# A new program order for the head of an mLSTM with two MoE layers: tables of due times, later gate matmuls, two more table loads

## The chip, the cores and the metric

The kernel runs on one core of one Trainium2 chip. The metric is the device time of one execution in microseconds (us). Five engines work side by side, each through its own list of instructions in order: PE (TensorE, matmuls), DVE (VectorE), ACT (ScalarE), POOL (GpSimd) and SP (SyncE, which here only issues DMAs). An instruction waits on semaphores until the work on other engines that it needs is done, and everything behind it on its engine waits with it.

## The reference

```python
# attention: B=2, H=8, S=768, D=40; state C (D x D) and n (D) for each batch and head
for t in range(S):
    m_new  = maximum(f_gate[t] + m, i_gate[t])
    f_stab = exp(f_gate[t] + m - m_new);  i_stab = exp(i_gate[t] - m_new);  m = m_new
    C = f_stab * C + i_stab * outer(v[t], k[t]);  n = f_stab * n + i_stab * k[t]
    y[t] = sigmoid(o_gate[t]) * (C @ q[t]) / maximum(abs(n . q[t]), 1)
x = y as (1536 tokens, 320)
# first MoE: 320 -> 2048 -> 320;  g(h) = h for h >= 1, 0 for h <= -1, (h + 1)^2 / 4 between
x = g(x @ w_in) @ w_out
# second MoE, the same sizes:  g(h) = max(h, 0) + log1p(exp(-abs(h)))
out = g(x @ w_in) @ w_out
```

## The kernel before

The recurrence is cut into 12 chunks of 64 steps. A chunk n needs a row of decays and gates, four groups of 32 small matmuls on PE, and work on DVE, ACT and POOL between them. In the order of one chunk, with the lines of the kernel before: `bc_n` (L564, PE: the running maxima `m_n`, L556, are spread over partitions by a matmul), the scan that makes the weights `f_n` from it (L590, DVE; L598 for later chunks), `qkp` (L518, PE: q times k), `f_n` times `qkp` (L620, DVE), `pv` (L505, PE: weights times values), the decay on q (L625, DVE: `qx` times `dec`), `inner` (L511, PE: state times q), `stp` (L526, PE: the chunk's part of the state), the denominators (L650, L653), the sigmoid (L645, ACT), sigmoid times denominators and `y_n` (L657, L660, DVE), the state's product with its decay (L669, POOL) and the sum (L678, DVE), and the transposes of `y_n` (L687, PE), which ACT copies out as `xh` (L692, L693) and DVE completes by the low part `xl` (L698, L700). The first matmuls of the MoE read `xh` and `xl`.

The running maxima of all steps come from two scans on DVE (L341: 16x256 for the first four chunks, 16x512 for the rest). The first four chunks (`EARLY = 4`) take their gates from rows on the chip; their decays go to DRAM (L393, `scr_d<-gd`) and come back spread over partitions as `dec` (L581, two tiles `dec0` and `dec1` in turn). The gates of the other eight come from eight matmuls into the PSUM tile D (L422), three subtractions and additions into `late` (L428), two exponentials (L432), a scan (L436), and two writes to DRAM. The exponentials and the sigmoid are in different activation tables, so between L432 and the first sigmoid stands one load of a table (L449).

The weights of the first MoE come in 32 pieces `raw` of 704 KB (ring of two); ACT turns each into `v` (L715, L719), DVE mends it (L726), ACT casts its high part `w` (L738), and DVE or POOL makes the low part (L747). An up-projection of 128 of the 2048 hidden units is eight matmuls (`h`, L767), named here h_0, h_1 and so on; its activation is three instructions (L775, L780, and L784 on DVE, which makes `u`), then the split `gh` (L816) and `gl` (L820), and a down-projection d_0, d_1 and so on of eight matmuls (L836 to L842). The second MoE is built likewise, with a softplus for activation.

The program order on each engine isn't written by hand. Every step is a task (`add`) with an engine, a cost, what it reads and writes, and a due time that is worked back from its successors; a class `Plan` runs a list scheduler over a model of the core (costs, DMA lanes, TensorE's two clock levels), and emits each instruction when the model starts it. 200 matmuls that compute nothing (`fill`, L460, `WARM`) are among the tasks: the scheduler puts them where PE would be idle ahead of the first up-projection. The choice on each engine is

```python
near = [i for i in q if begin[i] <= now]
...
i = min(near, key=lambda i: (due[i], i))
```

so a change of a due time, of a cost or of the time from which a task is `ready` can move everything behind it.

Of the kernel before, what the change touches and what calls it, by code (L numbers as in the profile page):

```python
# [20 lines left out]
C = 64  # L21
NC = S // C
# [13 lines left out]
class Plan:  # L36
# [44 lines left out]
    def run(self, start):  # L81
# [45 lines left out]
        for i in reversed(order):  # L127
            c = ts[i]["cost"] + ts[i]["after"] + self.LATENCY
            low = min((due[k] for k in succ[i]), default=clock) - c
            due[i] = low if due[i] is None else min(due[i], low)  # L130
        left = [len(d) for d in deps]
        ready = [t["hold"] for t in ts]
        queue, free = {}, {e: 0.55 for e in ("pe", "dve", "act", "pool", "sp")}
# [76 lines left out]
def mlstm_moe_moe(ctx: ExitStack, tc: tile.TileContext, gates, late, qk, tok, ident, w1, w2, out):  # L210
# [126 lines left out]
    for s, (c0, c1) in enumerate(SEG):  # L337
        a, b = c0 * C, c1 * C

        def t(a=a, b=b):  # L340
            nc.vector.tensor_tensor_scan(  # L341
                out=tiles["gm",][:, a + 1:b + 1], data0=gate("gf", a, b), data1=gate("gi", a, b),
                initial=tiles["gm",][:, a:a + 1], op0=ALU.add, op1=ALU.max)
        add("dve", scan(b - a), t, reads=[(gf, s), (gi, s), (gm, "z"), (gm, 0)], writes=[(gm, s)])

# [69 lines left out]

    def t():
        nc.vector.memset(col(4), 0.0)
    add("dve", 0.1, t, reads=[(LT, 0)], writes=[(LT, 4)])

    def t():  # L420
        for c in range(NC - EARLY):
            nc.tensor.matmul(  # L422
                banks[1][:, 2, 0:C + 1], tiles["gi",][0:16, S + 112 - 16 * c:S + 240 - 16 * c],
                tiles["gm",][:, n0 + C * c:n0 + C * c + C + 1], start=(c == 0), stop=(c == NC - EARLY - 1))
    add("pe", 0.9, t, duty=0.75, reads=[(gm, 1), (gm, 0), (gi, 1), (("bc", 1),)], writes=[(("D",), "s")], at=-50.5)
    for k, m, op in ((0, 0, ALU.add), (0, 1, ALU.subtract), (1, 1, ALU.subtract)):
        def t(k=k, m=m, op=op):
            nc.vector.tensor_tensor(out=col(k), in0=col(k), in1=banks[1][:, 2, m:m + C], op=op)  # L428
        add("dve", vec(C), t, reads=[(("D",), "s")], writes=[(LT, k)])
    for k in range(2):  # L430
        def t(k=k):
            nc.scalar.activation(out=col(k), in_=col(k), func=ACTF.Exp)  # L432
        add("act", act(C), t, reads=TAB, writes=[(LT, k)])

    def t():
        nc.vector.tensor_tensor_scan(  # L436
            out=col(5), data0=col(0), data1=col(4), initial=1.0, op0=ALU.mult, op1=ALU.add)
    add("dve", scan(C), t, reads=[(LT, 0), (LT, 4)], writes=[(LT, 5)])

    def t():  # L440
        nc.vector.memset(tiles[LT][:, 0:1], 0.0)
    add("dve", 0.07, t, reads=[(LT, 5)], writes=[(LT, 0)])
    for k, x, key in ((5, scr_d[1], (("scd",), 1)), (0, scr_f, (("scf",),))):
        def t(k=k, x=x):
            nc.sync.dma_start(out=x.rearrange("c r l -> (c r) l"), in_=col(k))
        add("sp", emit=t, reads=[(LT, k)], writes=[key], **dma(32))

    def t():
        nc.scalar.preload_act_table_set("sigmoid_and_others")  # L449
    add("act", 1.3, t, writes=TAB, due=20.0)  # L450


    def t():
# [88 lines left out]
    def attention(c, at):  # L542
# [79 lines left out]
        if c > 0:  # L622
            def t():
                q = tiles[QD][:, 1:3].rearrange("p b i l -> p (b i) l")
                nc.vector.tensor_tensor(out=q, in0=q, in1=tiles[DK], op=ALU.mult)  # L625
            add("dve", vec(512), t, port=True, reads=[*ATT, (DK,)], writes=[(QD,)])

# [28 lines left out]
        def t():  # L656
            nc.vector.scalar_tensor_tensor(  # L657
                out=hd(tiles[SG]), in0=tiles[DN].to_broadcast([128, H, D]), scalar=1.0, in1=hd(tiles[SG]),
                op0=ALU.min, op1=ALU.mult)
            nc.vector.tensor_tensor(  # L660
                out=new("y", Y, [128, DM]).rearrange("p (c i d) -> p c i d", c=2, d=D), in0=pv_view(n)[:, :, :, 0:D],
                in1=tiles[SG].rearrange("p (c i d) -> p c i d", c=2, d=D), op=ALU.mult)
        add("dve", 2 * vec(DM) + 0.1, t, port=True, reads=[*ATT, (P, "p"), (DN,)], writes=[(SG,), (Y, 0)],
            new=[("y", Y)])

# [38 lines left out]
    def weights(l, f):  # L704
# [17 lines left out]
        add("act", act(WC), t, reads=TAB, writes=[(V,)])  # L722

# [32 lines left out]
    def up(l, j, f, at):  # L756
# [3 lines left out]
        def t():  # L760
# [50 lines left out]
    def split_g(l, j, f, G):  # L811
# [6 lines left out]

        def t():
            nc.vector.tensor_tensor(  # L820
                out=new("gl", GL, [128, n], F32R), in0=tiles[G], in1=tiles[GH].bitcast(F32), op=ALU.subtract)
        add("dve", vec(n), t, port=True, reads=[(G,), (GH,)], writes=[(GL,)], new=[("gl", GL)])

    ACC, MIX = ("D",), ("A",)

    def down1(j, f, at):
# [5 lines left out]
        def t():  # L832
# [5 lines left out]
            for i in range(2):  # L838
# [41 lines left out]
    def down2(j, f, at):  # L880
# [181 lines left out]
```

## Time and profile before

| | us |
|---|---|
| time, median of 3 runs (lowest to highest) | 431.64 (430.56 to 433.64) |
| time of the profiled execution | 431.35 |
| its span in the profile | 429.5 |
| mean granted clock of TensorE over the span | 0.991 of full |

The span is the stretch from the first to the last instruction in the profile; the time of the same execution is 1.85 us longer. "Busy" is the time in which an engine worked on data; a matmul in the timeline has its start and its length, and in square brackets the time in which the engine stood idle before it and what ended that. The granted clock is a share of full speed; one half of it is TensorE's lower level.

### The profile page before, as it was taken

To read this page: it belongs to the slowest core of one execution; us is meant where nothing else is said; L and a number is where in the kernel's file an instruction comes from. 1 tells how busy PE (TensorE), PEld (TensorE's weight loads), DVE (VectorE), ACT (ScalarE), POOL (GpSimd) and SP (SyncE) were. 2 spreads that over 40 slices of the span, in tenths; PEclk is the share of its full clock that TensorE was granted. 3 is DMA by queue.
4 is the path that set the end of the run, shared out by engine and by line. 5 is a ranking of instruction groups with operands and counts; after the bars stand their busy time and mean duration, and the time that the engine had idled before them with its cause. 6 is when DMAs were issued, how large, how long until landed. Compare 5 with 4: busy or idle time off the path is not lost.

```text
span 429.5 us, 8096 instructions
## 1 busy us (share of the span) xinstructions
PE 409.7 (95%) x3299; PEld 340.3 (79%) x3299; DVE 295.2 (69%) x479; ACT 260.1 (61%) x447; POOL 37.2 (9%) x46
## 2 busy tenths in 40 slices
PE   7988779999899999999999999999999999999994
PEld 5555558877788888887888888999989999899994
DVE  4687998999868556556878787655565555655552
ACT  3255867768666446889889755555555555555551
POOL 3333122213101000000000000000000000000001
PEclk9999969999999999999999999999999999999999
DMA  8979595797912001644344000000020000110002
GB/s 289 343 260 318 156 295 177 213 321 221 304 66 74 2 2 51 193 162 136 134 134 137 0 2 0 1 2 0 2 61 2 0 2 0 36 27 2 0 2 61
DMA packets 13685, 44.93 MB, mean 105 GB/s; under 512 B 2320, under 2 KB 3984, under 8 KB 13648
## 3 DMA queue, kind: packets, MB, share of 16 engines
q1 hardware_dynamic: 12832, 43.22, 31.2%
q10 hardware_dynamic: 752, 1.03, 0.9%
q8 instruction: 26, 0.43, 0.4%
q0 software_dynamic: 64, 0.16, 0.2%
q14 instruction: 11, 0.09, 0.1%
HBM read 42.36 MB, written 2.05 MB: 103 GB/s over the span
## 4 chain that ended last, share of the span: by engine, by line
PE 77%; DMA 8%; DVE 6%; ACT 4%; issue 1%; SPq 1%; POOL 0%; DVEq 0%; POOLq 0%
PE h L767 36%; DMA raw<-in_w_dram 5%; PE D L841 4%; PE D L840 4%; PE D L842 4%; PE D L897 3%; PE D L899 3%; PE D L898 3%; PE A L898 3%; PE A L899 3%; PE A L897 3%; PE D L836 2%; PE D L837 2%; DMA f<-scr_f 2%; ACT v L715 1%
## 5 line engine op out<-in xcount | busy, mean ns | idle before, releaser
L767 PE MATMUL h<-xh,w 128*128 128x512 f32 x576 | 182.6, 400 | 1.5 <-DVE w L747 1.1
L767 PEld LDWEIGHTS h<-xh,w 128*128 128x128 f32 x576 | 108.7, 189 | 26.8 <-DVE w L747 3.0
L820 DVE TENSOR_TENSOR gl<-u,gh 128x512 fp32r<-128x512 f32 x96 | 67.5, 704 | 39.6 <-ACT gh L816 38.4
L816 ACT CAST gh<-u 128x512 fp32r<-128x512 f32 x96 | 59.4, 619 | 46.7 <-DVE u L807 34.0
L767 PE MATMUL h<-xl,w 128*128 128x512 f32 x192 | 76.3, 397 | 1.4 <-DVE xl L698 1.4
L807 DVE TENSOR_TENSOR u<-u,e 128x512 f32<-128x512 f32 x48 | 33.3, 693 | 29.2 <-ACT e L803 29.2
L803 ACT ACTIVATE e<-e 128x512 f32<-128x512 f32 x48 | 30.3, 632 | 37.6 <-DVE e L798 37.6
L775 ACT ACTIVATE u<-h 128x512 f32<-128x512 f32 x48 | 28.5, 595 | 25.9 <-PE h L767 25.6
L767 PEld LDWEIGHTS h<-xl,w 128*128 128x128 f32 x192 | 36.4, 190 | 8.0 <-DVE xl L698 1.8
L784 DVE SCALAR_TENSOR_TENSOR u<-u,h 128x512 f32<-128x512 f32 x48 | 32.7, 682 | 13.9 <-ACT u L780 13.7
L841 PE MATMUL D<-gh,w 128*128 128x512 f32 x96 | 37.9, 395 | 0.0
L840 PE MATMUL D<-gh,w 128*128 128x512 f32 x96 | 37.8, 394 | 0.0
L842 PE MATMUL D<-gl,w 128*128 128x512 f32 x96 | 37.5, 391 | 0.0
L798 DVE SCALAR_TENSOR_TENSOR e<-u,h 128x512 f32<-128x512 f32 x48 | 33.0, 687 | 6.0 <-ACT u L794 1.0
L726 DVE SCALAR_TENSOR_TENSOR v<-raw,v 128x704 int32<-128x704 int32 x32 | 28.6, 895 | 9.8 <-ACT v L719 8.8
L794 ACT ACTIVATE u<-h 128x512 f32<-128x512 f32 x48 | 28.7, 598 | 10.6 <-PE h L767 10.3
L747 DVE TENSOR_TENSOR w<-v,w 128x64 fp32r<-128x64 f32 (+2 forms) x45 | 30.2, 701 | 2.4 <-ACT w L738 2.4
L715 ACT ACTIVATE v<-raw 128x704 f32<-128x704 int8 x32 | 27.1, 849 | 7.3 <-DMA raw<-in_w_dram 5.4
L780 ACT ACTIVATE u<-u 128x512 f32<-128x512 f32 x48 | 30.2, 630 | 0.4
L897 PE MATMUL D<-w,gh 128*128 128x320 f32 x96 | 29.6, 309 | 0.1
L899 PE MATMUL D<-w,gl 128*128 128x320 f32 x96 | 29.7, 309 | 0.0
L898 PE MATMUL A<-w,gh 128*128 128x320 f32 x96 | 29.7, 309 | 0.0
(120 smaller groups left out, 611.5 us busy)
## 6 DMA issues: line engine op xcount, KB each, us to landing
raw<-in_w_dram SPq DMA_DIRECT2D x32, 704.0 KB, 4.8
qx<-in_qk_dram SPq DMA_DIRECT2D x12, 640.0 KB, 7.2
tok<-in_tok_dram SPq DMA_DIRECT2D x12, 496.0 KB, 6.0
dec<-scr_d SPq DMA_DIRECT2D x16, 128.0 KB, 6.7
f<-scr_f SPq DMA_DIRECT2D x16, 128.0 KB, 6.7
out_dram<-o SPq DMA_DIRECT2D x20, 80.0 KB, 2.1
dec<-scr_d ACTq DMA_DIRECT2D x6, 128.0 KB, 7.0
consts<-in_ident_dram SPq DMA_DIRECT2D x1, 164.0 KB, 4.0
```

Of the source, the lines that this page charges most:

```text
L767: nc.tensor.matmul(hp, a, x, start=(i == 0), stop=(i == len(ops) - 1))
L784: nc.vector.scalar_tensor_tensor(out=tiles[U], in0=tiles[U], scalar=1.0, in1=tiles[HP], op0=ALU.min, op1=ALU.max)
L798: nc.vector.scalar_tensor_tensor(out=new("e", E, [128, n]), in0=tiles[M], scalar=-2.0, in1=tiles[HP], op0=ALU.mult, op1=ALU.add)
L807: nc.vector.tensor_tensor(out=tiles[M], in0=tiles[M], in1=tiles[E], op=ALU.add)
L816: nc.scalar.copy(new("gh", GH, [128, n], F32R), tiles[G])
L820: nc.vector.tensor_tensor(out=new("gl", GL, [128, n], F32R), in0=tiles[G], in1=tiles[GH].bitcast(F32), op=ALU.subtract)
L840: nc.tensor.matmul(d[i], hi[:, k], gh, start=s, stop=False)
L841: nc.tensor.matmul(d[i], lo[:, k], gh, start=False, stop=False)
L842: nc.tensor.matmul(d[i], hi[:, k], gl, start=False, stop=e)
L897: nc.tensor.matmul(d, gh[:, k], hi, start=s, stop=False)
L898: nc.tensor.matmul(d, gh[:, k], lo, start=False, stop=False)
L899: nc.tensor.matmul(d, gl[:, k], hi, start=False, stop=e)
```

## The change

Two tables are added to the planner: `RANK` moves the due times of 41 tasks by up to 7.9 us either way, and `HOLD` the earliest starts of eight. Some costs of the model change (a fill, up- and down-projections, transposes, the late gate matmuls). The second scan of the maxima is held back to 7.6 us of the model's time. The block of the late gates becomes a function that is called ahead of chunk 3 and brings its own table load, so that ACT loads three tables where it loaded one after the first: sigmoid, exponentials, sigmoid. `warm`, which the fills read, is set on DVE and not on POOL. The weights of the first MoE no longer depend on the loaded table. The decay on q (L625) and `gl` (L820) may run on POOL, and sigmoid times denominators and `y` become two tasks.

```diff
+    RANK = {
+        10: 4.3, 19: -7.7, 230: -3.2, 245: 4.3, 248: -7.4, 249: -4.6, 268: 4.6, 280: 1.4, 287: -6.6, 291: 4.4,
...
+    HOLD = {
+        238: 6.2, 258: -4.8, 282: -5.2, 317: 5.5, 318: 7.3, 331: -4.9, 437: 5.0, 438: -2.9,
...
+        for i, d in self.RANK.items():
+            due[i] += d
...
-        ready = [t["hold"] for t in ts]
+        ready = [t["hold"] + self.HOLD.get(t["i"], 0.0) for t in ts]
...
-        add("dve", scan(b - a), t, reads=[(gf, s), (gi, s), (gm, "z"), (gm, 0)], writes=[(gm, s)])
+        add("dve", scan(b - a), t, reads=[(gf, s), (gi, s), (gm, "z"), (gm, 0)], writes=[(gm, s)], hold=7.6 * s)
...
-    add("pe", 0.9, t, duty=0.75, reads=[(gm, 1), (gm, 0), (gi, 1), (("bc", 1),)], writes=[(("D",), "s")], at=-50.5)
...
-    def t():
-        nc.scalar.preload_act_table_set("sigmoid_and_others")
-    add("act", 1.3, t, writes=TAB, due=20.0)
-
-
-    def t():
-        nc.gpsimd.memset(warm, 1.0)
-    add("pool", 0.46, t, writes=[(("warm",),)])
+    def table(name, hold=0.0):
+        def t():
+            nc.scalar.preload_act_table_set(name)
+        add("act", 1.3, t, writes=TAB, hold=hold)
+
+    table("sigmoid_and_others", 7.5)
+
+    def late_gates():
+        table("exp_and_others")
...
+        add("pe", 1.8, t, duty=0.75, reads=[(gm, 1), (gm, 0), (gi, 1)], writes=[(("D",), "s")], at=-30.5, hold=15.0)
...
+        table("sigmoid_and_others")
+
+
+    def t():
+        nc.vector.memset(warm, 1.0)
+    add("dve", 0.1, t, writes=[(("warm",),)])
...
-        add("pe", 0.25, t, fill=True, reads=[(("warm",),)], writes=[(("fill",),)], new=[("hb", ("fill",))] if i == 0 else [])
+        add("pe", 0.215, t, fill=True, reads=[(("warm",),)], writes=[(("fill",),)], new=[("hb", ("fill",))] if i == 0 else [])
...
-            add("dve", vec(512), t, port=True, reads=[*ATT, (DK,)], writes=[(QD,)])
+            add("dve|pool", vec(512), t, port=True, reads=[*ATT, (DK,)], writes=[(QD,)])
...
-        add("pe", 0.34, t, reads=[(Y, 0)], writes=[(TR,), (P, "s")], at=at[3])
+        add("pe", 0.45, t, reads=[(Y, 0)], writes=[(TR,), (P, "s")], at=at[3])
...
-        add("act", act(WC), t, reads=[(R,), *TAB] + ([*ATT] if l else []), writes=[(V,)], new=[(tag, V)])
+        add("act", act(WC), t, reads=[(R,)] + ([*ATT, *TAB] if l else []), writes=[(V,)], new=[(tag, V)])
...
-        add("pe", 8 * (n / 2400 + 0.013), t, reads=[(W, 0), (W, 1)] + xkeys(j), writes=[(HP,)], new=[(tag, HP)], at=at)
+        add("pe", 8 * (n / 2400 + 0.0185), t, reads=[(W, 0), (W, 1)] + xkeys(j), writes=[(HP,)], new=[(tag, HP)], at=at)
...
-        add("dve", vec(n), t, port=True, reads=[(G,), (GH,)], writes=[(GL,)], new=[("gl", GL)])
+        add("dve|pool", vec(n), t, port=True, reads=[(G,), (GH,)], writes=[(GL,)], new=[("gl", GL)])
...
     for n in range(NC):
+        if n == EARLY - 1:
+            late_gates()
         if n == EARLY:
             late_is()
         attention(n, where[n])
```

The lines of the changed kernel have other numbers: by 13 to 21 higher than before.

On ACT, from the cast of `gr` to the first sigmoids (`is_col` holds the gates as columns, `state` the first copy of the state), the kernel before has

```order
L378 CAST gr_128<-gf_142 16x256
L405 COPY is_col_129<-isp_0_200 64x2x8 x4
L393 DMA scr_d0_137<-gd_197 16x4x64
L581 DMA dec0_120<-scr_d0_137 64x512 x2
L581 DMA dec1_121<-scr_d0_137 64x512 x2
L432 ACTIVATE late_164<-late_164 128x64
L676 COPY state_130<-A_122 128x328
L432 ACTIVATE late_164<-late_164 128x64
L449 ACT_TABLE_LOAD
L645 ACTIVATE sig_0_339<-tok_0_155 128x320
```

and the changed kernel

```order
L391 CAST gr_128<-gf_142 16x256
L325 CAST sel_126<-consts_124 128x128
L418 COPY is_col_129<-isp_0_203 64x2x8 x4
L338 COPY id_h_125<-consts_124 128x512
L431 ACT_TABLE_LOAD
L664 ACTIVATE sig_0_240<-tok_0_160 128x320
L406 DMA scr_d0_137<-gd_201 16x4x64
L600 DMA dec0_120<-scr_d0_137 64x512 x2
L697 COPY state_130<-A_122 128x328
L664 ACTIVATE sig_1_322<-tok_1_208 128x320
L600 DMA dec1_121<-scr_d0_137 64x512 x2
```

The table load, a copy (`id_h`) and the first sigmoid now stand ahead of the decays' way to DRAM; the copy of the state and a sigmoid stand between the two pairs of `dec`; the exponentials of `late` have gone to a later place, behind `v` of the second weight.

On PE the eight gate matmuls (L422) stood before `bc_0`:

```order
L518 MATMUL A_122<-qx_0_151 64x64 x16
L399 MATMUL isp_0_200<-consts_124,gi_143 128x16 x2
L422 MATMUL D_123<-gm_148,gi_143 128x65 x8
L460 LDWEIGHTS warm_127
L460 MATMUL fill_162<-warm_127 128x512
L564 MATMUL bc_0_224<-m_0_216,sel_126 128x512
```

and are now in chunk 3 (there L444, between `inner` of chunk 2 and `pv` of chunk 3):

```order
L708 MATMUL D_123<-consts_124,y_1_481 64x128
L537 MATMUL D_123<-qx_3_310 64x64 x16
L530 MATMUL A_122<-state_130,qx_2_170 64x41 x16
L479 LDWEIGHTS warm_127
L479 MATMUL fill_151<-warm_127 128x512
L479 LDWEIGHTS warm_127
L479 MATMUL fill_151<-warm_127 128x512
L444 MATMUL D_123<-gm_148,gi_143 128x65 x8
L524 MATMUL D_123<-vi_3_454,f_3_381 64x41 x16
```

They moved behind the `xl` reads of tile D by chunk 1's transposes, and `pv` of chunk 3 follows them at once.

On PE, ahead of the transposes of chunk 4 (tr_4: L687, in the changed kernel L708), the kernel before has one up-projection, h_3, behind chunk 4's four groups, which stand behind h_0, h_1, h_2 and d_0:

```order
L505 MATMUL A_122<-vi_4_687,f_4_668 64x41 x16
L511 MATMUL A_122<-state_130,qx_4_446 64x41 x16
L518 MATMUL A_122<-qx_5_586 64x64 x16
L526 MATMUL A_122<-ve_4_758,tok_4_482 40x41 x16
L767 MATMUL h_0_0_3_852<-xh0_131,w_0_3_761 128x512
L767 MATMUL h_0_0_3_852<-xl0_134,w_0_3_761 128x512
L767 MATMUL h_0_0_3_852<-xh0_131,w_0_3_761 128x512 x2
L767 MATMUL h_0_0_3_852<-xl0_134,w_0_3_761 128x512
L767 MATMUL h_0_0_3_852<-xh0_131,w_0_3_761 128x512 x3
L687 MATMUL A_122<-consts_124,y_4_874 128x128 x2
```

In the changed kernel chunk 4's groups stand behind h_0 to h_3, d_0 and d_1, and d_2, h_5 and h_4 follow them before tr_4; its end is

```order
L863 MATMUL D_123<-gl_0_0_2_886,w_0_2_688 128x512
L788 MATMUL h_0_0_5_921<-xh0_131,w_0_5_892 128x512
L788 MATMUL h_0_0_5_921<-xl0_134,w_0_5_892 128x512
L788 MATMUL h_0_0_5_921<-xh0_131,w_0_5_892 128x512 x2
L788 MATMUL h_0_0_5_921<-xl0_134,w_0_5_892 128x512
L788 MATMUL h_0_0_5_921<-xh0_131,w_0_5_892 128x512 x3
L788 MATMUL h_0_0_4_935<-xh0_131,w_0_4_811 128x512
L788 MATMUL h_0_0_4_935<-xl0_134,w_0_4_811 128x512
L788 MATMUL h_0_0_4_935<-xh0_131,w_0_4_811 128x512 x2
L788 MATMUL h_0_0_4_935<-xl0_134,w_0_4_811 128x512
L788 MATMUL h_0_0_4_935<-xh0_131,w_0_4_811 128x512 x3
L708 MATMUL A_122<-consts_124,y_4_947 128x128 x2
```

So one up-projection and one down-projection more than before stand between `stp` of chunk 4 and tr_4, and one of each more ahead of chunk 4. Further on in the first MoE the same blocks are in other places too; later the order on PE is the same in both kernels.

## Rows read from the trace of the kernel before

**Rows 1.** The page, parts 1 and 2: engines' totals; granted clock in 40 slices.

```profile
PE 409.7 (95%) x3299; PEld 340.3 (79%) x3299; DVE 295.2 (69%) x479; ACT 260.1 (61%) x447; POOL 37.2 (9%) x46
...
PEclk9999969999999999999999999999999999999999
```

**Rows 2.** Three stretches: busy us of PE, PEld, DVE, ACT, POOL, then granted clock.

```profile
55.00:60.00 5.00, 2.81 (x8) 2.33 (x9) 4.85 (x9) 3.25 (x7) 1.59 (x3) 0.63 0.97 343
60.00:65.00 5.00, 5.00 (x17) 3.96 (x16) 4.96 (x10) 3.06 (x6) 0.00 (x0) 0.69 0.99 263
40.00:115.00 75.00, 67.59 (x868) 53.12 (x867) 66.16 (x115) 55.34 (x95) 14.95 (x15) 0.95 0.76 239
```

**Rows 3.** The waits of PE: us in total, times, the longest.

```profile
PE A L687 <- DVE state L678: 3.8, 2, 2.8
PE A L505 <- DVE f L620: 2.2, 2, 2.0
PE h L767 <- DVE xl L698: 1.4, 1, 1.4
PE h L767 <- DVE w L747: 1.1, 1, 1.1
```

**Rows 4.** PE's timeline up to 60 us: start, length, instruction.

```profile
1.92 2.32 PE L460 MATMUL fill<-warm 128*128 128x512 bf16 x5 [1.92 <-POOL warm L454]
...
6.57 3.65 PE L422 MATMUL D<-gm,gi 16*128 16x65 f32 x16
...
15.33 1.15 PE L526 MATMUL A<-ve,tok 64*64 64x41 f32 x32
...
24.51 0.68 PE L505 MATMUL A<-vi,f 64*64 64x41 f32 x32 [0.21 <-DVE f L620]
...
39.35 0.50 PE L767 MATMUL h<-xl,w 128*128 128x512 f32 x1 [1.36 <-DVE xl L698]
...
50.01 0.68 PE L505 MATMUL A<-vi,f 64*64 64x41 f32 x32 [1.96 <-DVE f L620]
...
57.19 0.90 PE L687 MATMUL A<-consts,y 128*128 128x128 f32 x3 [2.85 <-DVE state L678]
```

**Rows 5.** ACT's timeline up to 20 us.

```profile
7.41 0.34 ACTq L393 DMA_DIRECT2D scr_d<-gd  x1
...
12.66 2.51 ACTq L581 DMA_DIRECT2D dec<-scr_d  x4
...
16.52 0.43 ACT L676 COPY state<-A 128x328 f32<-128x328 f32 x1 [0.29 <-PE A L526]
...
17.12 1.28 ACT L449 ACT_TABLE_LOAD   x1
18.41 0.83 ACT L645 ACTIVATE sig<-tok 128x320 f32<-128x320 f32 x2
```

**Rows 6.** DVE's timeline up to 50 us.

```profile
15.78 0.54 DVE L428 TENSOR_TENSOR late<-late,D 128x64 f32<-128x64 f32 x3
...
21.77 1.21 DVE L590 TENSOR_TENSOR_SCAN f<-bc,id_h 128x512 f32<-128x512 f32 x1
22.90 0.67 DVE L625 TENSOR_TENSOR qx<-qx,dec 128x512 f32<-128x512 f32 x1
...
35.99 2.21 DVE L747 TENSOR_TENSOR w<-v,w 128x64 fp32r<-128x64 f32 x2
...
49.87 0.95 DVE L747 TENSOR_TENSOR w<-v,w 128x64 fp32r<-128x64 f32 x2
```

**Rows 7.** DMAs of `dec`: us from issue to landing.

```profile
DMA to landing us min/median/max: 4.4/6.6/9.3
```

**Rows 8.** DMA issues: queue, count, KB each, median us to landing.

```profile
scr_d<-gd ACTq DMA_DIRECT2D x1, 16.0 KB, 5.2
```

**Rows 9.** POOL's timeline, 30 to 50 us.

```profile
34.97 1.86 POOL L747 TENSOR_TENSOR w<-v,w 128x64 fp32r<-128x64 f32 x2 [0.17 <-ACT w L738]
```

**Rows 10.** The chain that ended last, 125 to 135 us.

```profile
129.88 1.87 PE h L767 x8
```

More of the change, by code (lines that the diff above doesn't have):

```diff
@@ L52 @@
     KEEP, IDLE = 0.8, 0.1
+    RANK = {
[5 rows of a table added]
+    }
+    HOLD = {
+        238: 6.2, 258: -4.8, 282: -5.2, 317: 5.5, 318: 7.3, 331: -4.9, 437: 5.0, 438: -2.9,
+    }
     def __init__(self, bufs):
@@ L414, in mlstm_moe_moe @@
     add("sp", emit=t, writes=[(LT, 0), (LT, 1)], new=[("w", LT)], **dma(64, "late"))
-    def t():
-        nc.vector.memset(col(4), 0.0)
-    add("dve", 0.1, t, reads=[(LT, 0)], writes=[(LT, 4)])
-    def t():
[L421 to L424, printed above, removed]
-    add("pe", 0.9, t, duty=0.75, reads=[(gm, 1), (gm, 0), (gi, 1), (("bc", 1),)], writes=[(("D",), "s")], at=-50.5)
@@ L426, in mlstm_moe_moe @@
[L426 to L433, printed above, removed]
-    def t():
-        nc.vector.tensor_tensor_scan(
-            out=col(5), data0=col(0), data1=col(4), initial=1.0, op0=ALU.mult, op1=ALU.add)
@@ L438, in mlstm_moe_moe @@
[L438 to L448, printed above, removed]
-        nc.scalar.preload_act_table_set("sigmoid_and_others")
@@ L450, in mlstm_moe_moe, with t @@
-    add("act", 1.3, t, writes=TAB, due=20.0)
-    def t():
-        nc.gpsimd.memset(warm, 1.0)
-    add("pool", 0.46, t, writes=[(("warm",),)])
+    def table(name, hold=0.0):
[6 more added lines that the diff above has]
+        def t():
+            nc.vector.memset(col(4), 0.0)
+        add("dve", 0.1, t, reads=[(LT, 0)], writes=[(LT, 4)])
+        def t():
+            for c in range(NC - EARLY):
+                nc.tensor.matmul(
+                    banks[1][:, 2, 0:C + 1], tiles["gi",][0:16, S + 112 - 16 * c:S + 240 - 16 * c],
+                    tiles["gm",][:, n0 + C * c:n0 + C * c + C + 1], start=(c == 0), stop=(c == NC - EARLY - 1))
+        add("pe", 1.8, t, duty=0.75, reads=[(gm, 1), (gm, 0), (gi, 1)], writes=[(("D",), "s")], at=-30.5, hold=15.0)
+        for k, m, op in ((0, 0, ALU.add), (0, 1, ALU.subtract), (1, 1, ALU.subtract)):
+            def t(k=k, m=m, op=op):
+                nc.vector.tensor_tensor(out=col(k), in0=col(k), in1=banks[1][:, 2, m:m + C], op=op)
+            add("dve", vec(C), t, reads=[(("D",), "s")], writes=[(LT, k)])
+        for k in range(2):
+            def t(k=k):
+                nc.scalar.activation(out=col(k), in_=col(k), func=ACTF.Exp)
+            add("act", act(C), t, reads=TAB, writes=[(LT, k)])
+        def t():
+            nc.vector.tensor_tensor_scan(
+                out=col(5), data0=col(0), data1=col(4), initial=1.0, op0=ALU.mult, op1=ALU.add)
+        add("dve", scan(C), t, reads=[(LT, 0), (LT, 4)], writes=[(LT, 5)])
+        def t():
+            nc.vector.memset(tiles[LT][:, 0:1], 0.0)
+        add("dve", 0.07, t, reads=[(LT, 5)], writes=[(LT, 0)])
+        for k, x, key in ((5, scr_d[1], (("scd",), 1)), (0, scr_f, (("scf",),))):
+            def t(k=k, x=x):
+                nc.sync.dma_start(out=x.rearrange("c r l -> (c r) l"), in_=col(k))
+            add("sp", emit=t, reads=[(LT, k)], writes=[key], **dma(32))
+        table("sigmoid_and_others")
@@ L622, in attention, with t @@
         if c > 0:
-            def t():
+            def t(e):
                 q = tiles[QD][:, 1:3].rearrange("p b i l -> p (b i) l")
-                nc.vector.tensor_tensor(out=q, in0=q, in1=tiles[DK], op=ALU.mult)
-            add("dve", vec(512), t, port=True, reads=[*ATT, (DK,)], writes=[(QD,)])
+                (nc.gpsimd if e == "pool" else nc.vector).tensor_tensor(out=q, in0=q, in1=tiles[DK], op=ALU.mult)
+            add("dve|pool", vec(512), t, port=True, reads=[*ATT, (DK,)], writes=[(QD,)])
         if not last:
@@ L659, in t @@
                 op0=ALU.min, op1=ALU.mult)
+        add("dve", vec(DM), t, port=True, reads=[*ATT, (DN,)], writes=[(SG,)])
+        def t():
             nc.vector.tensor_tensor(
@@ L662, in t @@
                 in1=tiles[SG].rearrange("p (c i d) -> p c i d", c=2, d=D), op=ALU.mult)
-        add("dve", 2 * vec(DM) + 0.1, t, port=True, reads=[*ATT, (P, "p"), (DN,)], writes=[(SG,), (Y, 0)],
-            new=[("y", Y)])
+        add("dve", vec(DM) + 0.03, t, reads=[*ATT, (P, "p"), (SG,)], writes=[(Y, 0)], new=[("y", Y)])
         if not last:
@@ L721, in t @@
                 alpha=2.0 ** 40)
-        add("act", act(WC), t, reads=TAB, writes=[(V,)])
+        add("act", act(WC), t, reads=TAB if l else (), writes=[(V,)])
         def t():
@@ L817, in split_g, with t @@
         add("act", act(n), t, reads=[(G,)], writes=[(GH,)], new=[("gh", GH)])
-        def t():
-            nc.vector.tensor_tensor(
+        def t(e):
+            (nc.gpsimd if e == "pool" else nc.vector).tensor_tensor(
                 out=new("gl", GL, [128, n], F32R), in0=tiles[G], in1=tiles[GH].bitcast(F32), op=ALU.subtract)
-        add("dve", vec(n), t, port=True, reads=[(G,), (GH,)], writes=[(GL,)], new=[("gl", GL)])
+        add("dve|pool", vec(n), t, port=True, reads=[(G,), (GH,)], writes=[(GL,)], new=[("gl", GL)])
     ACC, MIX = ("D",), ("A",)
@@ L842, in t @@
                 nc.tensor.matmul(d[i], hi[:, k], gl, start=False, stop=e)
-        add("pe", 8 * (n / 2400 + 0.013), t, reads=[(W, 0), (W, 1), (GH,), (GL,)], writes=[(ACC, i) for i in [0, 1, 2, *("qps" if first else "")]], at=at)
+        add("pe", 8 * (n / 2400 + 0.0185), t, reads=[(W, 0), (W, 1), (GH,), (GL,)], writes=[(ACC, i) for i in [0, 1, 2, *("qps" if first else "")]], at=at)
     def to_x(j):
@@ L899, in t @@
                 nc.tensor.matmul(d, gl[:, k], hi, start=False, stop=e)
-        add("pe", m * 3 * (DM / 2400 + 0.013), t, reads=[(W, 0), (W, 1), (GH,), (GL,)], writes=dk, at=at)
+        add("pe", m * 3 * (DM / 2400 + 0.0167), t, reads=[(W, 0), (W, 1), (GH,), (GL,)], writes=dk, at=at)
         if e:
```

4 rows, old and new, of the table RANK are left out of this document.

## The prediction

> **What bounds the kernel now.** I read the page first: PE is busy for 409.7 us of 429.5, and the granted clock is at its full level in 39 of 40 slices; the one that stands apart is the sixth, 54 to 64 us [rows 1]. So time can come only from PE's idle stretches and from that slice. The stretches say where: from 40 to 115 us PE is busy 67.59 of 75 us and VectorE 66.16 [rows 2], while behind that PE has almost no gaps (the whole list of PE's waits, of which [rows 3] are the largest, is short). So the change, which moves the first 60 us and a little of what follows, can win in two places: before the first up-projection gets going, at 39.35, where its wait for `xl` ends [rows 4], and between there and 115.
>
> What may be won after 39.35: PE waited 1.96 us for f_4's product at 50.01 and 2.85 us for state_4 at 57.19 [rows 4]; the group of L687 has one more wait, 3.8 less 2.8 = 1.0, and L767 waited 1.1 for a weight [rows 3]. That is 6.9 us. Then the clock: at 57.19 PE went back to work after 2.85 idle, and the granted clock of 55 to 60 is 0.63 and of 60 to 65 0.69 [rows 2]. At its lower level (one half) a share of 0.31 lost in the second stretch is 5 x 0.31 / 0.5 = 3.1 us, so the low clock ends near 63.1; from 57.19 that is 5.9 us in which 2.95 us of full-speed work were done. So 2.95 are lost. Together 9.85 us is the most that this stretch can give by its waits.
>
> What may be won before 39.35: the way to it goes over the decays. scr_d is issued at 7.41, its data lands 5.2 us later, at 12.6, and dec is issued at 12.66 (four in 2.51 us) [rows 5, 8]; dec takes 4.4 to 9.3 us to land [rows 7]; qx times dec of chunk 1 starts at 22.90 [rows 6]. Behind it on VectorE stand the products of chunks 1 to 3, whose y, transposes, xh and xl release the first up-projection.
>
> **The change part by part: the head.** On ACT the table load (1.28 [rows 5]) and sigma_0 now stand ahead of scr_d. The queue that issues DMAs is held up by the wait of sigma_0 for tok_0; I put the issue at 8.0 instead of 7.41 (an estimate: the load begins where is_col ended, near 7.8, and the DMA needs no result of it). Landing 5.2 later is 13.2, dec0 is issued at 13.3 and 13.9. The next copy (state, 0.43 [rows 5]) stands behind that pair and before the pair dec1, so dec1 no longer shares the lanes with dec0, and raw1 now waits for dec0 on SP. Landing by the middle value, 6.6, less a little for the emptier queues: 19.9; by the ends, 18.3 and 23.2 [rows 7]. The state's copy was at 16.52 because two `late` exponentials stood around it, whose input needed L422; these have gone. den_0, f_2's scan and y_0 then end by 17.5, and qx of chunk 1 starts at 19.9, 3.0 us before its old start.
>
> From there to the first xl, VectorE has other work than before. Ahead of qx stood f_3's scan (1.21) and the three `late` steps (0.54) [rows 6]; now they stand behind it, and so does the product of f_1 (at the length of the qx row, 0.67): +2.4. Against it, w_0's low part leaves VectorE for POOL: -0.95 by its ordinary row, -2.21 by the row at 35.99 [rows 6]; I take -1.3. The eight gate matmuls, 3.65 us at the lower clock [rows 4], now stand in chunk 3 with the product of f_3 waiting for them on VectorE, and v's mend, den_3, y_3 and all of xl behind that product. At full clock they cost half, 1.8, and fills stand ahead of them, so I take 1.4 exposed; the bounds are 0 (xh and the transposes of chunk 1 fill it) and 3.65. Two more table loads of 1.28 on ACT stand before v_0's second step and before sigma_3; in the order they lie between steps that wait for the first weights and for y, so I count them as hidden by those waits; if sigma_3 comes last behind them, they cost up to one load, 1.28. Sum of the head: -3.0 + 2.4 - 1.3 + 1.4 = -0.5. With the ends: the dec row moves it by -1.6 or +3.3, the gates by -1.4 or +2.2, so about -2.3 to +2.9 where not all fall on one side. More fills from the first microsecond (11 ahead of qk0 instead of 5, first start 1.92 [rows 4]) cost nothing where PE waits anyway for qx; the cover is that wait. If it is gone, six fills at 0.46 each (2.32 / 5) are 2.8.
>
> **After the first up-projection.** Before, chunk 4's four groups stood behind h_0 to h_2 and d_0, and only h_3 between its last group and its transposes. An up- or down-projection is 1.87 us [rows 10], a chunk's group 0.68 [rows 4]. So PE had 5 x 1.87 + 4 x 0.68 = 12.1 us of work where it took 57.19 - 39.35 = 17.8. Now it has h_0 to h_5 and d_0 to d_2 ahead of the transposes: 9 x 1.87 + 2.7 = 19.5 us. VectorE's work in 40 to 57 was 13.7 us, and one more hinge and one more split at 0.69 each make 15.1. So PE's work is longer than VectorE's here, and the 2.85 us wait with its 2.95 us of low clock has nothing to stand on: -5.8. The 1.96 us wait for f_4: chunk 4 is two blocks later, 3.7 us; the wait goes unless f_4's scan comes later too, which waits for dec, scr_f and two DMAs behind it that the later gates push back. I leave as much here: what PE gains in one place it waits in another, w_3, gl_0 or f_4, since VectorE now has 0.9 of its time full. So 2.0 stay here, and the two late waits (1.0 and 1.1) stay as well: 9.85 - 4.1 = 5.75 won, with bounds 0 (VectorE is the bound, below) and 9.85.
>
> POOL takes over qx of five chunks and gl of three blocks, at 0.68 each of VectorE's time, 5.4 us, about three of them in its fullest stretch. But the row says what a move may cost: while POOL worked on w_1 for 1.86 us from 34.97 [rows 9], VectorE's own w took 2.21 instead of 0.95 [rows 6]. That is 1.26 us for one neighbour. The Trainium skill, "SBUF — State Buffer", section on the two separate sides, says that VectorE and GpSimd share one port pair under an exclusive lock, so that an instruction with two SBUF inputs on VectorE stands still while GpSimd has it; the row agrees, and by that rule alone the eight moves, at 1.86 x 512 / 704 = 1.35 us each on POOL by the row, would cost up to 10.8 us of VectorE's time to free 5.4, which is rival C. Between that and a gain of 5.4 I take the moves at zero, since POOL is busy for 15 of the 75 us [rows 2] and many of VectorE's neighbours read PSUM.
>
> **The sum.** 431.35 (the profiled execution) - 0.5 - 5.75 = 425.1. The run is 0.3 below the median of three, and I don't correct for that.
>
> **The rivals.** (A) As above, 425.1: 0.45. (B) As above, but the gate matmuls and groups of chunk 3 come at the lower clock or dec lands late: +2.9 + 0.5 in place of -0.5 for the head, 428 to 429: 0.17. (C) VectorE is the bound: it is busy 66.16 of 75 us [rows 2], what PE does earlier it then waits for, and POOL's work holds it up as in [rows 6, 9]; then most of the 5.75 comes back as waits for u and gl, 429 to 431.6: 0.16. This is also the case in which the new order doesn't do what it is made for. (D) Slower: dec0 lands after 9.3 us, at 23.2, and PE, idle meanwhile, falls to the lower clock in the head: seven groups cost 1.15 instead of 0.68 (3.3), the gates 3.65 instead of 1.8, and qx starts 0.3 later than before instead of 3.0 earlier. 3.3 + 1.8 + 3.3 - 0.5 = +7.9 for the head, with half of what follows won (-3): 436; it decides from a landing of dec0 after 23 us. 432.5 to 438: 0.12. (E) Better: the late waits vanish as well (-2.1), and the head wins 2.3: 421.2: 0.10.
>
> A table load may cost ACT more than its 1.28: the sigmoid follows it at 18.41, where 17.12 + 1.28 ends [rows 5], so the row shows none. The Trainium skill, "ScalarE: Activation LUTs", section on what ACT_TABLE_LOAD costs, gives 2.66 us with a drain; by that, the two added loads would stand 2.7 us longer on ACT, of which I would expect half before xh, so some 426.5; the row speaks against the drain, and that this holds has a chance of 0.05, which lies inside A and B.
>
> **How the numbers follow.** The forecast is A, 425.1. The range leaves out about 1 in 10 on each side: below, E's outer half, so 420.5; above, D, so 432.5. A measurement of this kernel tells 1% (4.3 us) from no change. Faster than 427.3: A but a little of its upper edge (0.43), E (0.10) and the edge of B (0.03): 0.56. Within 1%, 427.3 to 436: the rest of B, C and a part of D: 0.34. Slower than 436: 0.10.
>
> **What would show it.** In the profile after: qx of chunk 1 on VectorE near 19.9; the gate matmuls near 30 us at 1.8 us, not 3.65; the first `xl` matmul of the MoE near 38.9; no wait of PE above 1 us before chunk 4's transposes and full clock in 55 to 65; one wait near 50 us of about 2 us. It is wrong if dec0 lands after 23, if the clock falls before 40 us, or if PE's waits for VectorE from 40 to 115 us sum up to more than 6.

## The result, and the profile after

The changed kernel is slower: 434.31 us in the median of 19 runs (431.67 to 436.85) against 430.99 of the kernel before (19 runs, 428.98 to 437.39), a ratio of 1.0073 with an interval of 1.0049 to 1.0097. That is less than the 1% that I took as a bound, but clear of noise. The forecast was 425.1, with a range of 420.5 to 432.5. Medians here and below are over all runs; ratios and their intervals leave out runs more than 1.5% above the fastest of the same kernel. The profiled execution took 435.12, its span is 433.3.

The page, parts 1 and 2 [rows 1]:

```profile
PE 413.9 (96%) x3313; PEld 341.8 (79%) x3313; DVE 292.8 (68%) x473; ACT 263.9 (61%) x449; POOL 47.4 (11%) x52
...
PEclk9956899999999999999999999999999999999999
```

The slice at 54 to 64 us that stood apart before is full now, as forecast; but the third to fifth, 22 to 54 us, are low. In all 19 runs the mean granted clock is 0.965 to 0.981. Stretches of 2 and 5 us say when (columns as in [rows 2]):

```profile
20.00:22.00 2.00, 0.08 (x4) 0.00 (x0) 0.29 (x1) 1.97 (x3) 0.00 (x0) 0.95 0.08 25
22.00:24.00 2.00, 0.94 (x36) 0.95 (x40) 2.00 (x3) 0.29 (x1) 0.00 (x0) 0.50 0.83 290
...
32.00:34.00 2.00, 1.55 (x52) 1.00 (x48) 0.95 (x4) 1.59 (x4) 1.59 (x2) 0.99 1.02 399
...
36.00:38.00 2.00, 1.09 (x32) 0.94 (x32) 1.19 (x3) 0.00 (x0) 0.15 (x1) 0.50 0.01 4
...
55.00:60.00 5.00, 4.46 (x18) 3.40 (x19) 4.44 (x7) 4.94 (x10) 0.91 (x1) 1.00 0.91 234
```

PE was idle from 20 to 23; from 22 the clock is at its lower level, comes back at 32, falls again at 35.5, during the gate matmuls (33.75 to 35.88), and is back at 45.7. One thing these rows don't show: the low clock of the first microseconds. In the kernel before the five fills at 1.92 take 2.32 us [rows 4], 0.46 each, and six fills at 34.74 take 1.46, 0.24 each, though its row for 5 to 10 us shows full clock. So a mean granted clock says nothing about the very start. PE's timeline shows what it waited for, and the new times of the places in [rows 4]:

```profile
19.39 0.68 PE L537 MATMUL A<-qx 40*64 40x64 f32 x30
23.05 1.10 PE L524 MATMUL D<-vi,f 64*64 64x41 f32 x32 [2.98 <-DVE f L639]
...
33.75 2.13 PE L444 MATMUL D<-gm,gi 16*128 16x65 f32 x16 [0.45 <-DVE xh L721]
36.73 1.09 PE L524 MATMUL D<-vi,f 64*64 64x41 f32 x32 [0.85 <-DVE f L639]
...
47.54 0.40 PE L788 MATMUL h<-xl,w 128*128 128x512 f32 x1
```

The wait of 2.98 us belongs to pv of chunk 1, for f_1's product. On VectorE that product stands behind the decay on q, which waits for dec0 [rows 6]:

```profile
21.71 0.69 DVE L644 TENSOR_TENSOR qx<-qx,dec 128x512 f32<-128x512 f32 x1 [3.86 <-DMA dec<-scr_d]
22.32 0.68 DVE L639 TENSOR_TENSOR f<-D,f 128x512 f32<-128x512 f32 x1
```

The two parts of the time come apart at the first `xl` matmul: 47.54 instead of 39.35, so the head is 8.2 us longer; from there to the end of the span it is 385.8 us instead of 390.15, 4.4 shorter. Between 47 and 120 us the largest waits, in the place of [rows 3], are now these (behind 120 one more of 1.0 for `w`):

```profile
PE A L708 <- DVE f L639: 1.9, 1, 1.9
PE h L788 <- DVE u L805: 0.8, 1, 0.8
...
PE h L788 <- DVE w L768: 0.3, 1, 0.3
```

### The profile page after: what moved, and what is told of

It reads as the page before. It is cut to its first block, busy times and chain, and to the rows that moved or that the text cites. A ratio compares the mean times of both kernels' runs of the same rounds, so it can differ in the third digit from the quotient of the medians.

```text
span 433.3 us, 8123 instructions
## 1 busy us (share of the span) xinstructions
PE 413.9 (96%) x3313; PEld 341.8 (79%) x3313; DVE 292.8 (68%) x473; ACT 263.9 (61%) x449; POOL 47.4 (11%) x52
## 4 chain that ended last, share of the span: by engine, by line
PE 76%; DMA 9%; DVE 8%; ACT 4%; issue 1%; SPq 1%; POOL 0%; ACTq 0%; DVEq 0%; POOLq 0%
PE h L788 35%; DMA raw<-in_w_dram 4%; PE D L862 4%; PE D L861 4%; PE D L863 4%; DMA dec<-scr_d 3%; PE A L919 3%; PE D L919 3%; PE D L920 3%; PE A L920 3%; PE D L918 3%; PE A L918 3%; PE D L857 2%; DVE w L768 2%; PE D L858 2%; PE fill L479 2%
## 5 line engine op out<-in xcount | busy, mean ns | idle before, releaser
L841 DVE TENSOR_TENSOR gl<-u,gh 128x512 fp32r<-128x512 f32 x93 | 64.8, 697 | 37.4 <-ACT gh L837 37.0
L828 DVE TENSOR_TENSOR u<-u,e 128x512 f32<-128x512 f32 x48 | 33.2, 693 | 29.2 <-ACT e L824 29.2
L796 ACT ACTIVATE u<-h 128x512 f32<-128x512 f32 x48 | 28.4, 593 | 20.5 <-PE h L788 19.9
L768 DVE TENSOR_TENSOR w<-v,w 128x704 fp32r<-128x704 f32 (+2 forms) x46 | 32.2, 729 | 2.6 <-ACT w L759 2.4
L747 DVE SCALAR_TENSOR_TENSOR v<-raw,v 128x704 int32<-128x704 int32 x32 | 29.7, 929 | 5.1 <-ACT v L740 5.1
L946 POOL DMA_DIRECT2D out_dram<-o x2 | 1.2, 616 | 272.9 <-ACT o L934 272.5
```

What stands on the lines that cost most here:

```text
L768: eng.tensor_tensor(out=w[:, o:o + b - a], in0=v[:, a:b], in1=w[:, a:b].bitcast(F32), op=ALU.subtract)
L828: nc.vector.tensor_tensor(out=tiles[M], in0=tiles[M], in1=tiles[E], op=ALU.add)
L841: (nc.gpsimd if e == "pool" else nc.vector).tensor_tensor(out=new("gl", GL, [128, n], F32R), in0=tiles[G], in1=tiles[GH].bitcast(F32), op= ...
```

## Experiments

All but one replay the planner's order and change only what is named (the one with more table loads changes what the task emits as well): "ahead a b" and "behind a b" put one task ahead of or behind another, "fills n a" puts n of the unused fill matmuls ahead of a task, "on" chooses the engine, "drop a b" takes out the fills between two tasks. The numbers are tasks: 256 f_1's product, 257 qx_1, 311 f_3's scan, 309 bc_3, 239, 260 and 319 pv of chunks 0, 1 and 3, 261 inner of chunk 1, 285 stp of chunk 2, 297 the gate matmuls, 427 isp_1. Ratios are to the kernel before, in the same series. The theories: (1) TensorE's clock is the loss of the head; (2) the place of dec0 and VectorE's order behind it are the loss by themselves; (3) the gates in chunk 3; (4) POOL's work holds VectorE up.

**f_1 first.**

```diff
+    EDITS = [("ahead", 256, 257), ("ahead", 311, 257)]
```

> The changed kernel with one edit: on VectorE the product of f_1 and the scan of f_3 stand ahead of the decay on q of chunk 1, which waits for dec0. Theory 1 (PE's 2.98 us wait for f_1 lets TensorE's clock fall, and the lower clock up to 45 us is the loss): no wait of more than about 2 us before 24, full clock up to the first up-projection, whose first xl matmul comes at 39 to 41 instead of 47.5; time 426 to 428.5. Theory 2 (the later dec0 and the order of VectorE behind it are the loss by themselves): PE only waits at the next group instead, the first xl matmul at 46 to 47.5, time 431.5 to 434.5.

Measured: 432.5, ratio 1.0012 (0.9977 to 1.0046), the first `xl` matmul at 46.08: a miss for theory 1, and by its time inside the range of theory 2. But the clock, which theory 1 wanted held, still fell, at 20 us, though the 2.98 us wait is gone. So the wait that I had singled out isn't needed for the fall: another, of 1.69 us for bc_3, came ahead of it. The stretch and the wait:

```profile
20.00:24.00 4.00, 4.00 (x124) 3.73 (x121) 2.19 (x6) 3.37 (x6) 0.11 (x1) 0.52 0.44 154
...
18.21 0.47 PE L607 MATMUL bc<-m,sel 128*128 128x512 f32 x1 [1.69 <-DVE f L633]
```

**12 fills in the gap.**

```diff
+    EDITS = [("fills", 12, 260)]
```

> The changed kernel with 12 more fill matmuls on PE ahead of pv of chunk 1, where PE stood idle for 2.98 us; nothing else moves, so every wait for dec0 and for VectorE stays as it is. Theory 1 (clock): full clock up to the first up-projection, first xl matmul at 39.5 to 42, time 427 to 429. Theory 2 (order and dec0): the fills change nothing that is waited for, first xl matmul at 46.5 to 48, time 433.5 to 435.

Measured: 430.96, ratio 1.0011 (0.9970 to 1.0052), the `xl` matmul at 44.72, between the two expectations. Work that computes nothing, on the engine that is waited for, takes 2.8 us off the head of the profiled execution. The clock now holds to 32.1 and falls there, in the middle of the gate matmuls; so theory 1 is right for the first fall and the forecast of its size was too high, since a second follows:

```profile
28.00:32.00 4.00, 3.56 (x82) 2.63 (x80) 1.88 (x5) 2.36 (x5) 1.36 (x2) 1.00 0.62 191
32.00:36.00 4.00, 2.64 (x41) 2.30 (x40) 1.53 (x4) 0.56 (x2) 2.38 (x3) 0.52 0.80 313
```

**Gates behind pv of chunk 3 as well.**

```diff
+    EDITS = [("fills", 12, 260), ("behind", 297, 319)]
```

> As the kernel with 12 fills, and the eight gate matmuls behind pv of chunk 3 instead of ahead of it, so that the product of f_3 on VectorE doesn't wait for them. Theory 1: the wait for the gates is no part of the loss once the clock holds, within 0.7 us of the kernel with the fills. Theory 3 (the gates in chunk 3 cost by themselves, and their wait lets the clock fall a second time near 36 us): 1.5 to 3 us faster than the kernel with the fills, and in that one the clock falls near 36.

Measured: 431.03, ratio 0.9974 (0.9922 to 1.0027), against the kernel with the fills alone not to be told apart. In the profile the second fall comes at 33.2 instead of 32.1, and `xl` at 42.47. Theory 3 gets at most a little: the wait for the gates moves, it doesn't go.

**POOL's moves back** (eight products and w_0 on VectorE).

```diff
+    EDITS = [("on", "dve", [316, 474, 493, 550, 568, 700, 756, 777, 336])]
```

> The changed kernel with the eight moved products and w_0 back on VectorE at the same place of the order. Theory 4 (POOL holds VectorE up, so that the moves cost more than they free): 1.5 to 4 us faster than the changed kernel, 430.5 to 433. Theory 1: the clock falls as before; the head moves by less than 1 us, and the 10 added instructions on VectorE cost 0 to 2 us behind 47 us: 434 to 436.

Measured: 433.25, ratio 1.0042 (1.0007 to 1.0078), between the two expectations and not to be told apart from the changed kernel's 1.0073; the clock is 0.972 to 0.984, as low as there. So this run decides nothing on POOL; its part comes back below.

**Holding the clock.**

```diff
+    EDITS = [("fills", 12, 260), ("behind", 297, 319), ("fills", 6, 319), ("fills", 3, 427)]
```

> The kernel with 12 fills and the gates behind pv of chunk 3, with 6 more fills ahead of pv of chunk 3 and 3 ahead of isp_1, where PE still waited 1.44 and 0.60 us and the clock fell at 33.4. Theory 1 (the clock is the whole loss of the head): full clock from the start up to the first up-projection, its first xl matmul at 38.5 to 40.5 (before: 39.35), time 425.5 to 428.5. Theory 2 (dec0 and the order behind it cost by themselves): the xl matmul stays at 41.5 or later though the clock is full, time 428.5 to 431.

Measured: 430.24, ratio 0.9965 (0.9927 to 1.0003). In the profiled execution the clock fell at 20, before the fills, with the same bc_3 wait of 1.7 us, and `xl` came at 44.89: inconclusive by its profile, and the median lies in theory 2's range. The twelve runs say more. The three with a mean clock of 0.998 or more took 427.5 to 428.4, theory 1's range, though f_1's product and dec0 stand as in the changed kernel; seven of the other nine, at 0.984 to 0.994, took 430.0 to 432.4, and two, at 0.990 and 0.993, 427.8 and 428.1 as well. So the clock sorts these runs in the main, not wholly.

**f_1 first and the clock held.**

```diff
+    EDITS = [("ahead", 256, 257), ("ahead", 311, 257), ("fills", 3, 309), ("fills", 6, 261), ("behind", 297, 319),
+             ("fills", 6, 319), ("fills", 3, 427)]
```

> The changed kernel with f_1's product and f_3's scan ahead of the decay on q of chunk 1, the gates behind pv of chunk 3, and fills where PE then waits: 3 ahead of bc_3, 6 ahead of inner of chunk 1, 6 ahead of pv of chunk 3, 3 ahead of isp_1. Theory 1 with the chain over dec0: full clock to the first up-projection, and 1.9 us of VectorE's work gone from the chain behind dec0: first xl matmul 1 to 2 us earlier than in the kernel that only holds the clock, at 37 to 39, time 424 to 427, below both kernels. If the chain isn't over dec0: no earlier than there.

Measured: 428.27, ratio 0.9942 (0.9907 to 0.9977): faster than both kernels, though slower than the 424 to 427 expected; in the profile the clock still fell, at 33.7 (0.72 from 32 to 36), and `xl` came at 41.92.

**Two more table loads** on top of that.

```diff
+            if not hold:
+                nc.scalar.preload_act_table_set(dict(exp_and_others="sigmoid_and_others").get(name, "exp_and_others"))
             nc.scalar.preload_act_table_set(name)
```

> As the kernel with f_1 ahead and the clock held, with each of the two added table loads doubled (four loads of 1.28 us instead of two). Theory 1 (the two loads lie in ACT's idle time): within 1 us of that kernel. Rival (a load is on the way of v_0 and sigma_3 and so of the first up-projection): 1.3 to 2.6 us slower.

Measured: 428.16, ratio 0.9933 (0.9897 to 0.9968), the same as without (0.9942), to within the intervals' 1.5 us. In this profile the clock held throughout (0.997) and `xl` came at 39.96. PE waited 1.2 us for y_3 there, whose sigmoid stands behind the second pair of loads, against 0.4 in the next kernel, which has single loads: doubled, that load comes near the path.

**All waits of the head filled.**

```diff
+    EDITS = [("ahead", 256, 257), ("ahead", 311, 257), ("fills", 6, 309), ("fills", 3, 239), ("fills", 6, 261),
+             ("fills", 2, 285), ("behind", 297, 319), ("fills", 6, 319), ("fills", 3, 427)]
```

> As the kernel with f_1 ahead and the clock held, with 8 more fills where PE still waited (6 ahead of bc_3 in place of 3, 3 ahead of pv of chunk 0, 2 ahead of stp of chunk 2). Theory 1: clock at 0.995 or more in every execution, first xl matmul near 40, time 426 to 428, 0.5 to 1.5 us below that kernel. If those waits aren't what lets the clock fall in some executions: the same as that kernel, 428.3.

Measured: 427.81, ratio 0.9898 (0.9858 to 0.9937), the lowest time, 1.0% below before. The clock is 0.993 to 0.999 in its six runs, a little under the 0.995 expected. PE's timeline, the same places as above:

```profile
30.36 2.00 PE L471 MATMUL D<-gm,gi 16*128 16x65 f32 x16
...
39.52 0.40 PE L815 MATMUL h<-xl,w 128*128 128x512 f32 x1
```

With the clock up the head ends at 39.52, where it ended before (39.35). What is left behind it is a wait for weights, which the changed kernel had for 0.3 us:

```profile
PE h L815 <- DVE w L795: 3.2, 5, 1.4
```

**The same with POOL's moves back**, all of them, and then only the seven of the later part (w_0 and the decay on q of chunk 3 stay on POOL).

```diff
+             ("on", "dve", [316, 474, 493, 550, 568, 700, 756, 777, 336])]
```

> As the kernel with 8 more fills, with the eight products and w_0 that went to POOL back on VectorE. Theory 4 (POOL's work holds VectorE up): 1.5 to 4 us faster than that kernel. Theory 1 and the forecast's zero for the moves: within 1.5 us of it.

```diff
+             ("on", "dve", [474, 493, 550, 568, 700, 756, 777])]
```

> As the kernel with 8 more fills, with the seven products of the later part (gl of three blocks, the decay on q of chunks 6, 7, 10 and 11) back on VectorE, and w_0 and the decay on q of chunk 3 left on POOL. If the moves of the head were worth the 3.4 us between the kernels with and without POOL's work (they kept VectorE's chain short and the clock up): the same as the kernel with 8 more fills, 427 to 428.5, with the first xl matmul near 39.5. If the moves of the later part were worth it: 430 to 431.5.

Measured: 431.24 with all back, ratio 0.9995 (0.9963 to 1.0027), slower than both expectations, and 428.86 with the later ones back, ratio 0.9899 (0.9865 to 0.9933), the same as with all on POOL (0.9898). So theory 4 is wrong: the later moves neither cost nor win more than the intervals' 0.4%, and the two of the head win about 1%. In the profile with all back the clock fell at 34.4 (0.80 from 32 to 36, 0.50 to 40) and `xl` came at 43.50; with two on POOL it held up to there, and `xl` came at 40.34.

**The kernel before without its fills** from bc_2 to the first up-projection (25 by the two profiles, 40 fills and 15; the expectation says 28).

```diff
+    EDITS = [("drop", 282, 660)]
```

> The kernel before without the 28 fills between bc_2 and the first up-projection; no other instruction moves. Theory 1 (it is the fills between the small groups that kept the clock up in the kernel before): the clock falls between 20 and 30 us, the first xl matmul comes 4 to 8 us later than 39.35, time 434 to 439. Theory 2: the fills do nothing here, 430.5 to 432.5.

Measured, in four runs: 437.37, ratio 1.0136 (1.0072 to 1.0201), `xl` at 43.24. Three runs have a clock of 0.961 to 0.968; the fourth shows 0.998 and is still the longest, 439.35, which stays unexplained. The profile shows the same fall in the kernel before, with no instruction moved that computes anything:

```profile
20.00:24.00 4.00, 3.17 (x68) 2.16 (x68) 3.93 (x6) 0.47 (x1) 0.84 (x1) 0.60 1.04 291
24.00:28.00 4.00, 3.05 (x81) 2.45 (x76) 2.73 (x7) 1.74 (x6) 2.18 (x3) 0.50 0.92 328
```

**The later part alone, in the kernel before**: chunk 4's transposes (439, with the copy 440) behind d_1 (673); then h_3 (681) ahead of chunk 4's groups (433) as well.

```diff
+    EDITS = [("behind", 439, 673), ("behind", 440, 439)]
```

> The kernel before with one edit: the transposes of chunk 4 on PE stand behind h_4 and d_1 instead of ahead of them (3.74 us of PE work between), as the change does with the head left alone. If the wait for state_4 and the low clock behind it are what the later part gives (the forecast's step): no wait of PE near 57, full clock from 55 to 65, 4 to 5.8 us faster than before, some 426 to 427.5. Rival (VectorE is the bound, the time comes back as waits for u, gl or a weight): within 1.5 us of before.

```diff
+    EDITS = [("ahead", 681, 433), ("behind", 439, 673), ("behind", 440, 439)]
```

> The kernel before with h_3 on PE ahead of chunk 4's four groups, and h_4 and d_1 between them and chunk 4's transposes: chunk 4 one block later, its transposes two. If the changed kernel's 4.4 us behind the first up-projection come from both waits (for f_4's product and for state_4) being covered together, with no fall of the clock between 50 and 65: no wait above 1.5 us from 45 to 65, 3 to 5 us faster than before, 427 to 429. Rival (the time comes back as waits at chunk 5, for weights or u, as with the transposes alone): within 1.5 us of before.

Measured: 434.46, ratio 1.0022 (0.9984 to 1.0061), and 433.33, ratio 1.0044 (1.0004 to 1.0085). Both of my expectations fell; the rival's, no gain, came true. In the first the wait for state_4 is gone (chunk 4's transposes start at 62.50 without one), but PE stood 2.7 us at 112, at chunk 8's group, and the clock fell all the same at 52, behind the wait for f_4 that had stayed. In the second the clock held from 36 to 70 and PE waited elsewhere:

```profile
51.87 0.50 PE L794 MATMUL h<-xh,w 128*128 128x512 f32 x1 [1.44 <-ACT w L765]
...
63.01 0.50 PE L794 MATMUL h<-xh,w 128*128 128x512 f32 x1 [1.67 <-DVE u L811]
...
77.44 0.73 PE L794 MATMUL h<-xh,w 128*128 128x512 f32 x2 [1.60 <-DVE w L774]
```

These two profiles show something else: the head of the kernel before, which neither edit touches, lost the clock in both, near 28 us and for 3.4 and 6.8 us, and `xl` came at 40.94 and 41.73 instead of 39.35. The second one's row:

```profile
28.00:32.00 4.00, 4.00 (x82) 3.25 (x81) 2.05 (x7) 1.20 (x4) 0.74 (x1) 0.50 0.51 91
```

So the old order has little margin too, and the 39.35 is one execution that held. The 31 runs of the kernel before in the first series, one program, spread from a clock of 0.983 to 1.000: the ten at 0.995 or more took 430.5 us in the mean, the five at 0.988 or less within the 1.5% took 433.3.

## Why the prediction was wrong

**The step that failed is the clock of the head.** The sum took 1.4 us for the gates "at full clock" and nothing for a fall; the fall stood in rival D, with a chance of 0.12, and "it decides from a landing of dec0 after 23 us". That condition was wrong: qx_1 could start at 21.71, 1.2 us earlier than before, and the clock fell nevertheless, before 40 us, which I had named as a sign of being wrong. That D's price agrees (+7.9 for the head, measured +8.2) is in part luck: it has 3.3 for a late qx_1, which came 1.8 later than forecast, and 1.8 for slow gates, which took 2.13 us. The prediction also took the row at 15.33 (1.15 us) for a group at the lower clock. That group takes 1.15 at full clock in the kernel with all waits filled and 1.93 at the lower one (40.53 in the changed kernel).

From 21.8 to 32 and from 35.5 to 45.7 us PE was busy for 17.6 us at half speed, so up to 8.8 us were lost there. How much of the 8.2 us that is by itself no run tells exactly, since none held the clock with the changed kernel's own order: fills alone took 2.8 us off the head, leaving fills out of the kernel before put 3.9 on, and in the kernels where `xl` came at 39.52 and 39.96 f_1 stands ahead and the gates behind pv of chunk 3 as well. That the order costs little beside the clock is suggested by the runs of **Holding the clock**: f_1 still stands behind qx_1, and the three with the highest clock took 427.5 to 428.4. My -0.5 for the rest of the head (38.85) is then wrong by a microsecond or so, not by eight.

**Why it falls.** I looked at the waits one by one and asked which of them end last. I had f_1's product behind qx_1 in the sum, at 0.67 us of VectorE's time; I didn't ask what PE would do meanwhile, which was nothing for 3 us. The planner put no fill there, though 146 of the 200 were left over: behind bc_2 the changed kernel has 23 fills and the kernel before 25, but none of the 23 lies between 17.8 and 24.9 us. "More fills from the first microsecond cost nothing" was true and beside the point. Nor is it that one wait: with f_1 ahead the clock fell behind the wait for bc_3, with the gap filled it fell at the gates.

That second fall has no long wait to go with it. With 12 fills PE waited at most 0.6 us at a time between 20 and 32, and was busy without a break from 31 on when the clock fell at 32.1. In six profiles (the changed kernel, f_1 first, 12 fills, gates behind, f_1 and hold, all moves back) it came during the eight gate matmuls or at most 0.7 us behind them; in four others they ran at full clock and the clock held. Whether the gates themselves bring it down wasn't tested, since no run takes them out of the head. What the runs show is that the head has little margin at several places, and that more fills there make the clock hold more often: 0.965 to 0.981 in the changed kernel, 0.973 to 0.990 with 12 fills, 0.991 to 1.000 with f_1 ahead and the fills, 0.993 to 0.999 with 8 more (0.989 to 1.000 with the later moves back on VectorE besides).

**dec0.** Forecast 19.9, measured 21.71; the range had 18.3 to 23.2. Issued at 13.59, 0.3 later than I said, it took 7.5 us.

**The gates.** 2.13 us in the changed kernel at a clock of nearly full, 2.00 in the best, where I wrote 1.8. VectorE waited 1.86 us for them, where I had 1.4.

**The table loads** are hidden, as forecast; doubling the two added ones didn't show in the time. The Trainium skill, "ScalarE: Activation LUTs", section on what ACT_TABLE_LOAD costs, gives 2.66 us with a drain; in the changed kernel the sigmoid follows its load of 1.28 us without one:

```profile
39.63 1.28 ACT L431 ACT_TABLE_LOAD   x1
40.92 0.47 ACT L664 ACTIVATE sig<-tok 128x320 f32<-128x320 f32 x1
```

**POOL.** Zero for the later moves was right. The head's two were in the sum at -1.3 (w_0), and measure about 1%; with them on VectorE the clock fell again in the profile, and how much of it is VectorE's own time the runs don't tell. The rule that the prediction took from the Trainium skill ("SBUF — State Buffer", section on the two separate sides), the lock between VectorE and GpSimd by which the moves would have cost more than they free, isn't seen in the times (0.9899 and 0.9898).

**Behind the first up-projection** I forecast -5.75 and the changed kernel has -4.4; both the wait for state_4 and the low clock at 57 are gone, as said, and so is f_4's wait, of which I had left 2.0 (0.2 at 61.30); 1.9 stand at 97.99 instead. But the same idea in the kernel before gave nothing, and its profiles show waits for weights and u in its place (rival C's mechanism). So which move brings the 4.4 stays open. In part they may be the head's loss given back: with its first up-projection 8.2 us late the changed kernel waited 1.3 us for weights in all, and the kernel whose head ends at 39.52 waited 3.2. Single executions don't show it, though: the one with `xl` at 39.96 waited 1.3 too. In the three profiles with the head at 39.5 to 40.3 the rest is 1.1 to 4.8 us shorter than before (389.1, 387.1 and 385.3 us). That, with a head no longer than before, is the 4 us of the best kernel; about 3 of them stay against those runs of the kernel before whose clock is 0.995 or more (430.8 in the mean of the same series, 427.7 for the best).

## What to carry to other kernels

A wait of TensorE can cost more than its length: 3 us of it were followed by 10 us at half clock here. For every move that makes TensorE idle, read which clock the stretch behind gets and price the move at both levels, also when no single wait is long, and read it in several executions, since one may hold where the next one falls. Filling matmuls belong where PE waits in the new order; how many there are elsewhere doesn't help. And a gain read from waits far behind a delayed start may not be a gain of its own: check whether it is still there when the start is back in its place.

## What was not expected

With the same instructions on TensorE up to 20 us, the clock fell in some executions and held in others: the kernel with 12 fills waited 1.66 us for bc_3 and kept it, the one with f_1 ahead waited 1.69 and lost it. The length of that wait itself varies with the first DMA's landing: on ACT the copy of the state stands behind the issue of dec0, which waits for scr_d, so an issue from 13.13 to 14.29 (best kernel) gives the copy at 14.39, and one from 14.07 to 16.01 (f_1 ahead) at 16.11 (the scan that the line names had ended at 15.10):

```profile
14.07 1.94 ACTq L624 DMA_DIRECT2D dec<-scr_d  x2
16.11 0.43 ACT L721 COPY state<-A 128x328 f32<-128x328 f32 x1 [5.87 <-DVE gm L378]
```
